# Attention with hashed buckets and two MLP blocks on one core: weight loads queued behind tile transposes, hash products in four column strips

## The chip, the cores and the metric

The kernel runs on one core of one Trainium2 chip. The time is device microseconds of one execution, the lower the better.

## The reference

Attention over 2 batches, 8 heads, 768 tokens, 64 numbers a head; a query sees the keys whose hash bucket is its own. Then a Fourier mixing with an MLP (weights w_ch1, w_ch2), then a gated MLP. The inputs are float32. The part around the change:

```python
q_bits = (np.einsum('bhsd,dk->bhsk', q, proj) > 0).astype(np.int64)
k_bits = (np.einsum('bhsd,dk->bhsk', k, proj) > 0).astype(np.int64)
mask = np.sum(q_bits * powers, axis=-1)[:, :, :, None] == np.sum(k_bits * powers, axis=-1)[:, :, None, :]
scores = np.where(mask, scale * np.matmul(q, k.transpose(0, 1, 3, 2)), -1000000000.0)
attn = np.exp(scores - np.max(scores, axis=-1, keepdims=True))
attn = attn / (np.sum(attn, axis=-1, keepdims=True) + 1e-09)
return np.matmul(attn, v)
...
un = (u - mu) / np.sqrt(var + 1e-06)
return u + np.maximum(un @ w_ch1, 0.0) @ w_ch2
```

## The kernel before

The 96 attention tiles (2 batches x 8 heads x 6 tiles of 128 queries) are worked one after the other by `attention`. For a tile, TensorE forms the scores (L387) into a tile s, VectorE takes their maximum (L397), ScalarE the exponential e (L399). Then e is split into an fp16 pair: a cast (L246, in batch 0 on GpSimd) and a subtract (L251, GpSimd); SyncE issues a transpose of the pair by DMA (L438), and three tiles later TensorE multiplies the result with V (L455 to L457). In batch 0, tiles 1 and 4 of each head go another way (`flip`): TensorE transposes e (L423).

Before a head, `prep_head` and `stacks` make its operands: q1 is a copy of x (queries above keys) scaled by qsc (L248 on VectorE, or L246 on GpSimd, as ENG says), k2 the remainder x qsc - q1 on VectorE (L258); three moves by DMA (L266) and one on GpSimd (L246) put the halves where TensorE wants them. Every two heads, `prep_group` loads x and v and forms the hash products z = zp x (L304, float32, each product in two passes), of which ScalarE takes the sign (L273); a product with the code table gives ct (L353), and ScalarE writes two blocks of rows from it (L280, L282) by which wrong buckets drop out of the scores.

`weight` prepares an MLP matrix. The matrices w1 and w2 hold 64-bit floats: a piece of them is loaded as pairs of 32-bit words into a buffer `wide` (L215, on SyncE's queue, 1 MB for w1, 512 KB for w2), VectorE turns it into float32 in three steps (L219, L220, L221), ScalarE sums the squares (L223), and at the end ScalarE and VectorE write the fp16 pair (L232, L234). There are three buffers `wide` for w1 and two for w2. w1 runs beside batch 0, w2 beside batch 1, w_in and w_out beside the second MLP product of batch 1.

`build` interleaves these streams by weights (`_merge`), and the framework's scheduler orders each engine's instructions from that; an engine runs its own in that order, and SyncE's queue carries every load, move and transpose. s, ct, z and the tile tp of `flip` share one ring of two-bank PSUM buffers (three in batch 0, two later); `pp` is a pool of one-bank tiles.

Of the kernel before, what the change touches and what calls it, by code (L numbers as in the profile page):

```python
# [9 lines left out]
F32 = mybir.dt.float32  # L10
FR = mybir.dt.float32r
F16 = mybir.dt.float16
I32 = mybir.dt.int32
AF = mybir.ActivationFunctionType
ALU = mybir.AluOpType
# [3 lines left out]
B, H, S, D = 2, 8, 768, 64  # L19
DM, DF, DG = 512, 2048, 1024  # L20
P = 128
NT = S // P
HT = NT // 2
HS = S // 2
NB = 6
GH = 2
# [22 lines left out]
NX = 4  # L49
W3 = 0.4  # L50
PEND = 5
BITS = 'A'
WB = (3, 2)
ENG = ({'oh': 'A', 'hi': 'D', 'mv': 'SSPS', 'cast': 'P', 'sub': 'P'}, {'oh': 'A', 'hi': 'P', 'mv': 'SSPS', 'cast': 'AAP', 'sub': 'P'})
GP = ''
FULL = (3, 11)
ZP = (False, False)
CP = (False, False)
ENG0 = {'hi': 'D', 'mv': 'AASA', 'oh': 'A'}
W_ATT0 = 1.5  # L60
# [41 lines left out]
class Kern:  # L102
    def __init__(self, tc, I, out):
        self.tc, self.nc, self.I, self.out = tc, tc.nc, I, out
        self.W = {}


    def rsqrt(self, pool, x, n):
# [42 lines left out]
    def setup(self, ctx):  # L151
        tc, nc, I = self.tc, self.nc, self.I
        self.cp = cp = ctx.enter_context(tc.tile_pool(name="const", bufs=1))
        self.ident = cp.tile([P, P], F32, tag="ident", name="ident")
        self.ones = cp.tile([P, P], F32, tag="ones", name="ones")
        self.codes = cp.tile([P, GH, P], F16, tag="codes", name="codes")
        self.pops = cp.tile([P, 2], F32, tag="pops", name="pops")
        pr = cp.tile([P, NB], F32, tag="pr", name="pr")
        nc.scalar.dma_start(out=pr, in_=I["proj"])
        nc.scalar.dma_start(out=self.codes, in_=I["codes"])  # L160
        nc.scalar.dma_start(out=self.pops, in_=I["pops"])
        nc.scalar.dma_start(out=self.ident, in_=I["ident"])
        self.zp = cp.tile([P, GH, 2 * GH * NB], F32, tag="zp", name="zp")
        nc.vector.memset(self.zp, 0.0)
        for hl in range(GH):
            for n in range(2):
                r = slice(64 * n, 64 * n + 64)
                o = NB * (2 * hl + n)
                nc.vector.tensor_copy(self.zp[r, hl, o:o + NB], pr[r])
        self.bits = []  # L170
        for i in range(2):
            t = cp.tile([P, S], F16, tag=f"bits{i}", name=f"bits{i}")
            nc.gpsimd.memset(t, 0.0)
            self.bits.append(t)
        nc.vector.memset(self.ones, 1.0)
        self.qsc = cp.tile([P, 1], F32, tag="qsc", name="qsc")
        nc.vector.memset(self.qsc[0:64], SCALE)
        nc.vector.memset(self.qsc[64:128], 1.0)
        self.XU = [cp.tile([P, NT, DM], F32, tag=f"xu{b}", name=f"xu{b}") for b in range(B)]

        def col(n):
            return cp.tile([P, 1], F32, tag=n, name=n)

        self.sc = {nm: (col(f"s_{nm}"), col(f"i_{nm}")) for nm in ("w1", "w2", "in", "sg", "out")}
        self.sg_ = [[(col(f"sv{b}{g}"), col(f"iv{b}{g}")) for g in range(NG)] for b in range(B)]
        self.iv1 = [[col(f"iw{b}{g}") for g in range(NG)] for b in range(B)]
        for t in sum(self.iv1, []):
            nc.gpsimd.memset(t[64:65], 1.0)
        self.sx = [(col(f"sx{b}"), col(f"ix{b}")) for b in range(B)]
        self.vq = [cp.tile([P, NG], F32, tag=f"vq{b}", name=f"vq{b}") for b in range(B)]  # L190
        self.prod = col("prod")
        self.tok = [cp.tile([P, NT], F32, tag=f"tok{b}", name=f"tok{b}") for b in range(B)]
        self.tiny = col("tiny")
        nc.gpsimd.memset(self.tiny, -1e-37)


    def weight(self, pool, nm, src, regions, spare, c, q):

        nc = self.nc
        wide = src.dtype == mybir.dt.int64  # L200
        src = src.bitcast(I32) if wide else src
        sub = WSUB.get(nm, 4)
        m = c // sub
        n = len(regions)
        s, i = self.sc[nm]
        acc = pool.tile([P, 8], F32, tag="wacc", name="wacc", bufs=1)
        tot = pool.tile([P, 1], F32, tag="wm", name="wm", bufs=1)
        for j in range(n):
            if not wide:
                q.dma_start(out=regions[j], in_=src[:, j * c:(j + 1) * c])  # L210
                yield 0.3
            for hf in range(sub if wide else 0):
                o = j * c + hf * m
                x = self.stp.tile([P, 2 * m], I32, tag="wide", name="wide", bufs=self.wb)
                q.dma_start(out=x, in_=src[:, 2 * o:2 * (o + m)])  # L215
                xv = x.rearrange("p (n w) -> p n w", w=2)
                lo, hi = xv[:, :, 0], xv[:, :, 1]
                t = regions[j][:, hf * m:(hf + 1) * m].bitcast(I32)
                nc.vector.tensor_scalar(out=t, in0=hi, scalar1=3, scalar2=0x3FFFFFFF, op0=ALU.logical_shift_left, op1=ALU.bitwise_and)  # L219
                nc.vector.scalar_tensor_tensor(out=t, in0=hi, scalar=-0x40000000, in1=t, op0=ALU.bitwise_and, op1=ALU.bitwise_or)  # L220
                nc.vector.scalar_tensor_tensor(out=t, in0=lo, scalar=29, in1=t, op0=ALU.logical_shift_right, op1=ALU.bitwise_or)  # L221
                yield 0.0029 * m
            nc.scalar.activation(spare[:, 0:c], regions[j], AF.Square, accum_out=acc[:, j:j + 1])  # L223
            yield 0.0005 * c
        nc.vector.tensor_reduce(tot, acc[:, 0:n], axis=AX.X, op=ALU.add)
        self.norm_pow2(tot, 2.0 ** 54, s, i, self.pc if nm == "w2" else None)
        yield 1.0
        views = []
        dst = spare
        for j in range(n):  # L230
            d = dst[:, 0:c].bitcast(F16).rearrange("p (t c) -> p t c", t=2)
            nc.scalar.activation(d[:, 0, :], regions[j], AF.Copy, scale=i)  # L232
            yield 0.0005 * c
            nc.vector.scalar_tensor_tensor(out=d[:, 1, :], in0=regions[j], scalar=i, in1=d[:, 0, :], op0=ALU.mult, op1=ALU.subtract)  # L234
            views.append(d)
            dst = regions[j]
            yield 0.0005 * c
        self.W[nm] = views
        self.spare = dst
# [28 lines left out]
                self.copy(e, to.bitcast(FR), fr)  # L268
        return (q1, k1), (q2, k2)

    def to_bits(self, out, z):
        if BITS == "A":
            self.nc.scalar.activation(out, z, AF.Sign, bias=self.tiny[0:24])  # L273
        else:
            self.nc.vector.tensor_scalar(out=out, in0=z, scalar1=0.0, scalar2=None, op0=ALU.is_gt)

    def one_hot(self, eng, qo, ko, c):

        nc = self.nc
# [6 lines left out]
    def prep_group(self, ap, vp, n, G):  # L286

        nc, I = self.nc, self.I
        b, g = divmod(n, NG)
# [6 lines left out]
        nc.sync.dma_start(out=v, in_=I["v"][b, g])  # L296
        yield
        bits = self.bits[n % 2]
        to = bits[0:24].rearrange("p (a c) -> p a c", a=2)
        z = None if ZP[b] else self.ps.tile([P, 2, 512], F32, tag="s", name="z")  # L300
        for hf in range(2):
            zh = self.pp.tile([P, 512], F32, tag="p", name="z")[:, 0:HS] if ZP[b] else z[:, hf, 0:HS]
            for hl in range(GH):
                nc.tensor.matmul(zh[0:24], self.zp[:, hl, :], xs[hl][:, hf * HS:(hf + 1) * HS], start=hl == 0, stop=hl == GH - 1)  # L304
            if ZP[b]:
                self.to_bits(to[:, hf], zh[0:24])
        if not ZP[b]:
            self.to_bits(to, z[0:24, :, 0:HS])
        yield
        vf = v.rearrange("p a b c -> p (a b) c")[:, :, 0:64]  # L310
        V = ap.tile([P, GH, NT, 130], F16, tag="V", name="V", bufs=2)
# [48 lines left out]
    def attention(self, ap, eps):  # L360

        nc = self.nc
# [66 lines left out]
        def rest(i):  # L429
            if flips(i):  # L430
                flip(i)
                return
            x = st[i]
            ep, EB = pick(i)
            c = ENG[i // (H * NT)]["sub"]
            self.sub(c[i % len(c)], x["eh"][:, 1, :], x["e"], x["eh"][:, 0, :])
            x["et"] = et = ep.tile([P, 2 * NT, P], F16, tag="et", name="et", bufs=EB[2])
            nc.sync.dma_start_transpose(out=et, in_=x["eh"].rearrange("p a c -> p (a c)"))  # L438

        def av(i):  # L440
            g, hl, qt = where(i)
# [373 lines left out]
    def build(self):  # L815
# [3 lines left out]
        with ExitStack() as ctx:  # L819
# [48 lines left out]
            def second():  # L868
                yield from att
                c_att.close()  # L870
                c_s2.close()
                pp3 = c_ps.enter_context(tc.tile_pool(name="pp3", bufs=4, space=PSUM))
                self.pp = Alt(pp, pp3, pp3, pp2, pp3, pp3)
                up = ctx.enter_context(tc.tile_pool(name="up", bufs=1))
# [31 lines left out]
def _tables():  # L906
# [22 lines left out]
    codes = np.zeros((P, GH, P), np.float16)  # L929
    sign = np.where((np.arange(64)[None, :] >> np.arange(NB)[:, None]) & 1, 1.0, -1.0)  # L930
    for hl in range(GH):
        codes[12 * hl:12 * hl + 6, hl, 0:64] = sign
        codes[12 * hl + 6:12 * hl + 12, hl, 64:128] = sign
    pop = (sign > 0).sum(0).astype(np.float32)
    pops = np.zeros((P, 2), np.float32)
    if BITS == "A":
        pop = np.full_like(pop, NB)
    pops[0:64, 0] = BIG * (1.0 - pop)
    pops[64:128, 0], pops[64:128, 1] = pop, -pop
    return {  # L940
# [45 lines left out]
```

## Time and profile before

| | us |
|---|---|
| median of 3 runs | 726.32 (720.83 to 726.87) |
| profiled execution | 724.48 |
| its span | 722.7 |
| TensorE, VectorE busy | 645.0 (89%), 503.9 (70%) |
| ScalarE, GpSimd busy | 329.8 (46%), 273.7 (38%) |

The profile names engines PE (TensorE matmul), PEld (its weight loads), DVE (VectorE), ACT (ScalarE), POOL (GpSimd) and SP (SyncE). A row of a group of instructions reads: line, engine, operation, output<-inputs, shapes, count | busy us, mean ns of one | idle time of the engine before them and what ended it. A row of a timeline reads: start, length in us, then the instruction. The span ends with the last instruction; the execution's time has some 2 us around it.

### The profile page before, as it was taken

To read this page: it belongs to the slowest core of one execution; us is meant where nothing else is said; L and a number is where in the kernel's file an instruction comes from. 1 tells how busy PE (TensorE), PEld (TensorE's weight loads), DVE (VectorE), ACT (ScalarE), POOL (GpSimd) and SP (SyncE) were. 2 spreads that over 40 slices of the span, in tenths; PEclk is the share of its full clock that TensorE was granted. 3 is DMA by queue.
4 is the path that set the end of the run, shared out by engine and by line. 5 is a ranking of instruction groups with operands and counts; after the bars stand their busy time and mean duration, and the time that the engine had idled before them with its cause. 6 is when DMAs were issued, how large, how long until landed. Compare 5 with 4: busy or idle time off the path is not lost.

```text
span 722.7 us, 12521 instructions
## 1 busy us (share of the span) xinstructions
PE 645.0 (89%) x4828; PEld 421.8 (58%) x4828; DVE 503.9 (70%) x1095; ACT 329.8 (46%) x517; POOL 273.7 (38%) x232
## 2 busy tenths in 40 slices
PE   3788987976876578999999999979999999999997
PEld 0666677764563357658865766736668444444443
DVE  6999598658999997745435694867562266777663
ACT  5766687764664556745632421423642044222110
POOL 2568588879486465536455041000000012111000
PEclk8899999996886879999999999989999999999999
DMA  8969787999798989737563036552000012011334
GB/s 310 312 182 213 140 175 143 204 202 259 158 235 169 212 193 211 140 67 152 101 128 108 2 60 221 125 148 91 1 1 1 1 35 53 15 29 18 86 88 117
DMA packets 182428, 92.24 MB, mean 128 GB/s; under 512 B 166240, under 2 KB 167008, under 8 KB 181344
## 3 DMA queue, kind: packets, MB, share of 16 engines
q1 hardware_dynamic: 181792, 91.30, 55.0%
q8 instruction: 38, 0.62, 0.4%
q10 hardware_dynamic: 576, 0.14, 0.1%
q14 instruction: 22, 0.18, 0.1%
HBM read 39.50 MB, written 3.15 MB: 59 GB/s over the span
## 4 chain that ended last, share of the span: by engine, by line
PE 56%; DVE 21%; DMA 12%; POOL 4%; issue 3%; ACT 2%; SPq 0%; DVEq 0%; POOLq 0%; ACTq 0%
PE c L674 13%; PE c L657 12%; PE gi L739 9%; PE sg L762 6%; PE s L387 4%; PE go L779 4%; DMA wide<-w_in 3%; DMA et<-eh 3%; DMA wide<-w 3%; DVE nm L397 2%; DVE w L221 2%; DVE w L220 2%; POOL eh L251 2%; DVE k L258 1%; PE y L542 1%
## 5 line engine op out<-in xcount | busy, mean ns | idle before, releaser
L251 POOL TENSOR_TENSOR eh<-e,eh 128x768 f16<-128x768 f32 x80 | 143.4, 1796 | 53.7 <-ACT eh L244 51.0
L657 PE MATMUL c<-unT,w 128*128 128x256 f16 x1152 | 136.8, 277 | 4.2 <-DVE h L664 4.2
L674 PE MATMUL c<-w,h 128*128 128x512 f16 x576 | 131.8, 384 | 5.3 <-DVE xu L678 5.3
L657 PEld LDWEIGHTS <-w 128*128 128x128 f16 x1152 | 113.0, 99 | 22.6 <-issue 5.3
L387 PE MATMUL s<-k,q 128*128 128x384 f32 x384 | 108.1, 413 | 17.8 <-ACT k L282 7.4
L399 ACT ACTIVATE e<-s,nm 128x768 f32<-128x768 f32 x96 | 85.3, 896 | 55.3 <-DVE nm L397 44.7
L397 DVE TENSOR_REDUCE nm<-s 128x1 f32<-128x768 f32 x96 | 90.3, 948 | 22.6 <-PE s L387 21.5
L674 PEld LDWEIGHTS <-h 128*128 128x128 f16 x576 | 56.2, 99 | 69.6 <-issue 9.2
L755 POOL TENSOR_TENSOR vh<-gv,vh 128x512 f16<-128x512 f32 x12 | 13.9, 1156 | 214.0 <-ACT vh L754 214.0
L387 PEld LDWEIGHTS s<-k,q 128*128 128x128 f32 x384 | 72.0, 211 | 30.1 <-ACT k L282 8.3
L455 PE MATMUL pav<-V,et 128*128 128x65 f16 x480 | 56.4, 199 | 19.2 <-DMA et<-eh 13.8
L664 DVE SCALAR_TENSOR_TENSOR h<-c,h 128x256 f16<-128x256 f32 x96 | 39.8, 419 | 36.3 <-ACT h L663 35.8
L246 POOL TENSOR_SCALAR eh<-e 128x768 f16<-128x768 f32 x48 | 47.9, 999 | 36.8 <-ACT e L399 30.7
L455 PEld LDWEIGHTS <-et 128*128 128x128 f16 x480 | 46.0, 102 | 26.1 <-DMA et<-eh 17.7
L456 PE MATMUL pav<-V,et 128*128 128x64 f16 x480 | 56.2, 197 | 0.0
L457 PE MATMUL pav<-V,et 128*128 128x65 f16 x480 | 56.2, 199 | 0.0
L456 PEld LDWEIGHTS <-et 128*128 128x128 f16 x480 | 46.5, 101 | 7.7 <-issue 6.9
L739 PE MATMUL gi<-in,xT 128*128 128x512 f16 x216 | 50.5, 379 | 0.0
L663 ACT ACTIVATE h<-c 128x256 f16<-128x256 f32 x96 | 34.6, 377 | 34.6 <-PE c L657 34.2
L739 PEld LDWEIGHTS <-xT 128*128 128x128 f16 x288 | 28.2, 98 | 35.0 <-issue 1.1
L457 PEld LDWEIGHTS <-et 128*128 128x128 f16 x480 | 46.5, 101 | 1.5 <-issue 0.8
L762 PE MATMUL sg<-vh,sg 128*128 128x512 f16 x180 | 40.8, 379 | 0.0
(198 smaller groups left out, 1009.9 us busy)
## 6 DMA issues: line engine op xcount, KB each, us to landing
wide<-w SPq DMA_DIRECT2D x8, 1024.0 KB, 8.9
wide<-w SPq DMA_DIRECT2D x16, 512.0 KB, 4.3
x<-qk SPq DMA_DIRECT2D x16, 384.0 KB, 4.5
k<-q SPq DMA_DIRECT2D x26, 192.0 KB, 4.1
wide<-w_in SPq DMA_DIRECT2D x16, 256.0 KB, 3.5
vst<-v SPq DMA_DIRECT2D x8, 396.0 KB, 5.3
y<-ot SPq DMA_DIRECT2D x12, 256.0 KB, 2.3
q<-q SPq DMA_DIRECT2D x13, 192.0 KB, 3.9
```

The source lines that it names most:

```text
L246: self.nc.gpsimd.tensor_scalar(out=out, in0=src, scalar1=scale, scalar2=1.0, op0=ALU.mult, op1=ALU.mult)
L251: (self.nc.vector if eng == "D" else self.nc.gpsimd).tensor_tensor(out=out, in0=a, in1=b, op=ALU.subtract)
L387: nc.tensor.matmul(s[:, hf, 0:HS], q[:, qs], k[:, hf * HS:(hf + 1) * HS], start=n == 0, stop=n == len(pairs) - 1)
L397: nc.vector.tensor_reduce(nm, x["s"], axis=AX.XY, op=ALU.max, negate=True)
L399: nc.scalar.activation(e.rearrange("p (a c) -> p a c", a=2), x["s"], AF.Exp, bias=nm)
L455: nc.tensor.matmul(pv[:, qt, 0:65], et[:, kb, :], V[:, hl, kb, 64:129], start=kb == 0, stop=False)
L456: nc.tensor.matmul(pv[:, qt, 0:64], et[:, kb, :], V[:, hl, kb, 0:64], start=False, stop=False)
L457: nc.tensor.matmul(pv[:, qt, 0:65], et[:, NT + kb, :], V[:, hl, kb, 64:129], start=False, stop=kb == NT - 1)
L657: nc.tensor.matmul(ps[:, 0:step], w[:, a, fo], uT[:, 4 * u + kc, o * P:o * P + step], start=m == 0, stop=m == 11)
L674: nc.tensor.matmul(ps, hs[n, f][:, a, j * P:(j + 1) * P], wv[:, w, :], start=f + m == 0, stop=f == NF - 1 and m == 2)
L739: nc.tensor.matmul(ps, xT[:, 4 * a + kc, :], w_in[kc][:, w, half * DM:(half + 1) * DM], start=n == 0, stop=n == 11)
L762: nc.tensor.matmul(ps, w_sg[kt][:, w, t * P:(t + 1) * P], vh[b][:, kt, a, :], start=n == 0, stop=n == 17)
```

## The change

Loads: `weight` asks for piece k+1 before it works on piece k (for w1, w2, and also w_in and w_out, which go through the same code), and while attention runs each load is put behind the newest tile transpose in SyncE's order. Hash products: zp is now 32 columns wide, and the four products of a group write four strips of 32 partitions of one bank from `pp`; the sign is taken in two instructions of 64 partitions. The code table follows. The scaled copy q1 (and its half-height form for head 3) of batch 0 goes to GpSimd, except for head 0.

```diff
-ENG = ({'oh': 'A', 'hi': 'D', 'mv': 'SSPS', 'cast': 'P', 'sub': 'P'}, ...)
+ENG = ({'oh': 'A', 'hi': 'P', 'mv': 'SSPS', 'cast': 'P', 'sub': 'P'}, ...)
...
+        def load(k):
+            if k >= n * sub:
+                return None
+            x = self.stp.tile([P, 2 * m], I32, tag="wide", name="wide", bufs=self.wb)
+            with ExitStack() as es:
+                if self.lastT is not None:
+                    es.enter_context(self.tc.issue_after(self.lastT))
+                q.dma_start(out=x, in_=src[:, 2 * m * k:2 * m * (k + 1)])
+            return x
+
+        nxt = load(0) if wide else None
...
-                o = j * c + hf * m
-                x = self.stp.tile([P, 2 * m], I32, tag="wide", name="wide", bufs=self.wb)
-                q.dma_start(out=x, in_=src[:, 2 * o:2 * (o + m)])
+                x, nxt = nxt, load(j * sub + hf + 1)
...
-        to = bits[0:24].rearrange("p (a c) -> p a c", a=2)
-        z = None if ZP[b] else self.ps.tile([P, 2, 512], F32, tag="s", name="z")
+        z = self.pp.tile([P, 512], F32, tag="p", name="z")
         for hf in range(2):
-            zh = self.pp.tile([P, 512], F32, tag="p", name="z")[:, 0:HS] if ZP[b] else z[:, hf, 0:HS]
             for hl in range(GH):
-                nc.tensor.matmul(zh[0:24], self.zp[:, hl, :], xs[hl][:, hf * HS:(hf + 1) * HS], start=hl == 0, stop=hl == GH - 1)
-            if ZP[b]:
-                self.to_bits(to[:, hf], zh[0:24])
-        if not ZP[b]:
-            self.to_bits(to, z[0:24, :, 0:HS])
+                r = 32 * (GH * hf + hl)
+                nc.tensor.matmul(z[r:r + 32, 0:HS], self.zp, xs[hl][:, hf * HS:(hf + 1) * HS], start=True, stop=True)
+        for hf in range(2):
+            r = slice(64 * hf, 64 * hf + 64)
+            nc.scalar.activation(bits[0:64, hf * HS:(hf + 1) * HS], z[r, 0:HS], AF.Sign, bias=self.tiny[r])
...
-            nc.sync.dma_start_transpose(out=et, in_=x["eh"].rearrange("p a c -> p (a c)"))
+            self.lastT = nc.sync.dma_start_transpose(out=et, in_=x["eh"].rearrange("p a c -> p (a c)")).ins
...
                 c_s2.close()
+                self.lastT = None
```

What the change moves, by the engines' orders. First VectorE at the first tiles of batch 0, before:

```order
L221 SCALAR_TENSOR_TENSOR w_2_150<-wide,w_2_150 128x1024
L328 SCALAR_TENSOR_TENSOR V<-vst,iv_94,V 128x12x64
L219 TENSOR_SCALAR w_3_151<-wide 128x1024
L220 SCALAR_TENSOR_TENSOR w_3_151<-wide,w_3_151 128x1024
L397 TENSOR_REDUCE nm<-s 128x1
L221 SCALAR_TENSOR_TENSOR w_3_151<-wide,w_3_151 128x1024
L397 TENSOR_REDUCE nm<-s 128x1 x3
```

and in the changed kernel at the same place (line numbers are those of its own file):

```order
L229 SCALAR_TENSOR_TENSOR w_2_148<-wide,w_2_148 128x1024
L328 SCALAR_TENSOR_TENSOR V<-vst,iv_92,V 128x12x64
L397 TENSOR_REDUCE nm<-s 128x1 x6
L266 SCALAR_TENSOR_TENSOR k_508<-x,qsc,q_505 128x768
L397 TENSOR_REDUCE nm<-s 128x1
L227 TENSOR_SCALAR w_3_149<-wide 128x1024
```

The third piece of w1 (w_3) stood around the first maximum nm, and now comes after the seventh. Next SyncE's queue over the first heads, before:

```order
L215 DMA wide<-w 128x2048 x3
L438 DMA_TRANSPOSE et<-eh 128x12x128 x3
L266 DMA k_504<-q_503 64x768
L438 DMA_TRANSPOSE et<-eh 128x12x128
L266 DMA q_505<-q_503 64x768
L266 DMA k_506<-q_503 64x768
L438 DMA_TRANSPOSE et<-eh 128x12x128
L293 DMA x<-qk 128x768
L215 DMA wide<-w 128x2048 x2
```

and after:

```order
L298 DMA vst<-v 128x792 x2
L438 DMA_TRANSPOSE et<-eh 128x12x128
L214 DMA wide<-w 128x2048
L438 DMA_TRANSPOSE et<-eh 128x12x128 x2
L214 DMA wide<-w 128x2048
L274 DMA k_506<-q_505 64x768
L274 DMA q_507<-q_505 64x768
L438 DMA_TRANSPOSE et<-eh 128x12x128 x2
L274 DMA k_508<-q_505 64x768
L214 DMA wide<-w 128x2048
```

Before, six of the eight loads of w1 stand ahead of the first transpose and the other two together behind the fifth; now two stand ahead of it, and the other six singly behind the 1st, 3rd, 5th, 7th, 9th and 11th. Last GpSimd around the operands of one head, before:

```order
L246 TENSOR_SCALAR eh<-e 128x768 x2
L251 TENSOR_TENSOR eh<-e,eh 128x768 x2
L246 TENSOR_SCALAR eh<-e 128x768
L246 TENSOR_SCALAR q_505<-k_506 64x768
L251 TENSOR_TENSOR eh<-e,eh 128x768
```

and after:

```order
L254 TENSOR_SCALAR eh<-e 128x768
L254 TENSOR_SCALAR q_505<-x,qsc 128x768
L259 TENSOR_TENSOR eh<-e,eh 128x768
L254 TENSOR_SCALAR eh<-e 128x768
L254 TENSOR_SCALAR q_507<-k_508 64x768
```

The scaled copy of x, which was VectorE's L248, is now a GpSimd instruction among the casts and subtracts of the running tiles.

## Rows read from the trace of the kernel before

**Rows 1.** Stretches: from:to us, length, busy PE, PEld, DVE, ACT, POOL, PEclk, DMA, GB/s
```profile
25.00:65.00 40.00, 32.40 (x279) 25.92 (x280) 37.78 (x40) 25.60 (x38) 30.09 (x21) 0.91 0.88 213
...
85.00:125.00 40.00, 34.36 (x369) 28.99 (x367) 36.79 (x53) 32.75 (x43) 32.13 (x23) 0.96 0.78 153
165.00:280.00 115.00, 82.26 (x699) 56.45 (x699) 108.03 (x167) 60.91 (x94) 74.69 (x58) 0.80 0.92 207
280.00:722.00 442.00, 431.84 (x2964) 262.31 (x2962) 266.80 (x756) 153.69 (x267) 85.19 (x69) 0.99 0.33 77
```

**Rows 2.** Groups of VectorE's instructions, 22 to 165 us
```profile
L234 DVE SCALAR_TENSOR_TENSOR w<-w,i_w,w 128x1024 f16<-128x1024 f32 x8 | 13.7, 1718 | 0.0
L220 DVE SCALAR_TENSOR_TENSOR w<-wide,w 128x1024 int32<-128x1024 int32 x5 | 10.9, 2180 | 0.0
L221 DVE SCALAR_TENSOR_TENSOR w<-wide,w 128x1024 int32<-128x1024 int32 x6 | 9.9, 1653 | 0.0
L258 DVE SCALAR_TENSOR_TENSOR k<-x,qsc,q 128x768 fp32r<-128x768 f32 x7 | 9.6, 1365 | 0.0
L248 DVE TENSOR_SCALAR q<-x,qsc 128x768 fp32r<-128x768 f32 x5 | 7.1, 1412 | 0.1
...
L219 DVE TENSOR_SCALAR w<-wide 128x1024 int32<-128x1024 int32 x5 | 4.1, 820 | 0.5 <-DMA wide<-w 0.5
```

**Rows 3.** The tile q: count, shortest/median/longest in ns, first and last start
```profile
L258 DVE SCALAR_TENSOR_TENSOR k<-x,qsc,q x14: 1002/1018/2098, 5.4 to 333.1; 128x768 fp32r<-128x768 f32 x14
...
L246 POOL TENSOR_SCALAR q<-k x13: 823/829/1798, 8.1 to 334.7; 64x768 fp32r<-64x768 f32 x13
L248 DVE TENSOR_SCALAR q<-x,qsc x7: 612/1256/1999, 4.2 to 121.9; 128x768 fp32r<-128x768 f32 x7
L246 POOL TENSOR_SCALAR q<-x,qsc x7: 904/907/1315, 134.8 to 332.1; 128x768 fp32r<-128x768 f32 x7
```

**Rows 4.** Timeline of the first tiles, 18.5 to 24.5 us
```profile
19.04 0.69 DVE L219 TENSOR_SCALAR w<-wide 128x1024 int32<-128x1024 int32 x1 [0.84 <-DMA wide<-w]
19.77 1.23 DVE L220 SCALAR_TENSOR_TENSOR w<-wide,w 128x1024 int32<-128x1024 int32 x1
...
21.89 0.90 ACT L399 ACTIVATE e<-s,nm 128x768 f32<-128x768 f32 x1 [1.75 <-DVE nm L397]
...
24.14 0.88 ACT L399 ACTIVATE e<-s,nm 128x768 f32<-128x768 f32 x1
```

**Rows 5.** Groups of GpSimd's instructions, 22 to 165 us
```profile
L251 POOL TENSOR_TENSOR eh<-e,eh 128x768 f16<-128x768 f32 x35 | 64.9, 1860 | 1.9
L246 POOL TENSOR_SCALAR eh<-e 128x768 f16<-128x768 f32 x33 | 33.3, 1012 | 22.5 <-ACT e L399 22.4
L246 POOL TENSOR_SCALAR q<-k 64x768 fp32r<-64x768 f32 x7 | 8.0, 1145 | 9.8 <-DVE k L258 5.1 <-issue 2.4 <-PE z L304 2.4
L246 POOL TENSOR_SCALAR q<-x,qsc 128x768 fp32r<-128x768 f32 x2 | 1.8, 906 | 1.1 <-PE s L387 1.1
```

**Rows 6.** The tile eh, as rows 3
```profile
L251 POOL TENSOR_TENSOR eh<-e,eh x80: 1632/1648/2732, 23.8 to 374.9; 128x768 f16<-128x768 f32 x80
L246 POOL TENSOR_SCALAR eh<-e x48: 821/830/1808, 22.9 to 374.0; 128x768 f16<-128x768 f32 x48
```

**Rows 7.** Timeline of VectorE and GpSimd at 90 and at 103 us
```profile
90.10 1.28 DVE L234 SCALAR_TENSOR_TENSOR w<-w,i_w,w 128x1024 f16<-128x1024 f32 x1
90.34 1.72 POOL L246 TENSOR_SCALAR q<-k 64x768 fp32r<-64x768 f32 x1 [2.27 <-DVE k L258]
...
102.46 2.50 POOL L251 TENSOR_TENSOR eh<-e,eh 128x768 f16<-128x768 f32 x1
103.51 1.87 DVE L248 TENSOR_SCALAR q<-x,qsc 128x768 fp32r<-128x768 f32 x1
```

**Rows 8.** Timeline of TensorE, the second group's hash products
```profile
29.56 2.76 PE L304 MATMUL z<-x,zp 128*24 128x384 f32 x8
```

**Rows 9.** Page, DMA issues: count, KB each, median us to landing
```profile
wide<-w SPq DMA_DIRECT2D x8, 1024.0 KB, 8.9
```

More of the change, by code (lines that the diff above doesn't have):

```diff
@@ L51 @@
 PEND = 5
-BITS = 'A'
 WB = (3, 2)
-ENG = ({'oh': 'A', 'hi': 'D', 'mv': 'SSPS', 'cast': 'P', 'sub': 'P'}, {'oh': 'A', 'hi': 'P', 'mv': 'SSPS', 'cast': 'AAP', 'sub': 'P'})
+ENG = ({'oh': 'A', 'hi': 'P', 'mv': 'SSPS', 'cast': 'P', 'sub': 'P'}, {'oh': 'A', 'hi': 'P', 'mv': 'SSPS', 'cast': 'AAP', 'sub': 'P'})
 GP = ''
 FULL = (3, 11)
-ZP = (False, False)
 CP = (False, False)
@@ L162, in setup @@
         nc.scalar.dma_start(out=self.ident, in_=I["ident"])
-        self.zp = cp.tile([P, GH, 2 * GH * NB], F32, tag="zp", name="zp")
+        self.zp = cp.tile([P, 32], F32, tag="zp", name="zp")
         nc.vector.memset(self.zp, 0.0)
[L165 to L169, printed above, removed]
+        for n in range(2):
+            r = slice(64 * n, 64 * n + 64)
+            nc.vector.tensor_copy(self.zp[r, NB * n:NB * n + NB], pr[r])
         self.bits = []
@@ L269, in stacks @@
         return (q1, k1), (q2, k2)
[L271 to L275, printed above, removed]
     def one_hot(self, eng, qo, ko, c):
@@ L871, in second @@
                 c_s2.close()
+                self.lastT = None
                 pp3 = c_ps.enter_context(tc.tile_pool(name="pp3", bufs=4, space=PSUM))
@@ L931, in _tables @@
     for hl in range(GH):
-        codes[12 * hl:12 * hl + 6, hl, 0:64] = sign
-        codes[12 * hl + 6:12 * hl + 12, hl, 64:128] = sign
+        codes[32 * hl:32 * hl + 6, hl, 0:64] = sign
+        codes[32 * hl + 6:32 * hl + 12, hl, 64:128] = sign
     pop = (sign > 0).sum(0).astype(np.float32)
     pops = np.zeros((P, 2), np.float32)
-    if BITS == "A":
-        pop = np.full_like(pop, NB)
+    pop = np.full_like(pop, NB)
     pops[0:64, 0] = BIG * (1.0 - pop)
```

## The prediction

> **What bounds the kernel now.** I read the table of stretches first. In the first 165 us the attention of batch 0 runs, with w1 being unpacked beside it; up to about 280 us the attention of batch 1, the first Fourier part and the unpacking of w2; from 280 us on TensorE is busy 431.84 of 442 us [rows 1], at 0.99 of full clock. That last stretch is TensorE's own work, and the change touches little of it, so a gain must come from what ends before 280 us, and it then reaches the end whole. In 165 to 280 us VectorE is busy 108.03 of 115 us: it sets that stretch. In the batch 0 stretches no engine is full by itself: VectorE 37.78 and 36.79 of 40 us, TensorE 32.40 and 34.36, GpSimd 30.09 and 32.13 [rows 1].
>
> Next I read the groups of GpSimd and VectorE instructions between 22 us (GpSimd's first tile) and 165 us, and beside them the shortest time that each form took anywhere. The mean is far above the shortest: the scaled copy q on VectorE has a mean of 1.412 us there [rows 2] and a shortest of 0.612 [rows 3]; the second step of the unpacking has 2.180 [rows 2] against 1.23 at the start [rows 4]; GpSimd's subtract 1.860 [rows 5] against 1.632 [rows 6]. The timeline shows why. At 90.10 VectorE starts a weight remainder of 1.28 us; GpSimd's copy, started at 90.34 and of 0.82 us when alone [rows 3], ends only 1.72 us later. At 102.46 GpSimd's subtract takes 2.50, and VectorE's q copy behind it at 103.51 takes 1.87 instead of 0.61 [rows 7]. The two engines take turns: an instruction of the one stretches by the rest of the other's. VectorE's 37.78 of 40 us is therefore largely waiting for GpSimd.
>
> So I add the undisturbed times of both as one resource, for 22 to 165 us. GpSimd: 35 subtracts of 1.63, 33 casts of 0.82, 7 copies of 0.82 and 2 of 0.90 [rows 3, 5, 6], 57.1 + 27.1 + 5.7 + 1.8 = 91.7 us. VectorE, leaving out what reads scores from PSUM: 8 remainders of 1.28 [rows 2, 7], 5 and 6 unpacking steps of 1.23, 5 first steps of 0.69 [rows 2, 4], 7 remainders k2 of 1.00 and 5 copies q of 0.61 [rows 2, 3], 10.2 + 13.5 + 3.5 + 7.0 + 3.1 = 37.3 us. Together 129.0 of 143 us, 90%. I take this pair, not VectorE, as the bound of the batch 0 stage.
>
> The Trainium skill ("SBUF — State Buffer", section "Who interferes with whom") says the same and gives the reason: VectorE in its two-port modes, or with two SBUF inputs, and GpSimd share one pair of ports, and whoever starts first holds it for the whole instruction while the other fully blocks. The trace agrees (the 1.72 us copy above). By that rule the move of q to GpSimd, below, costs 1.5 us; were there no such lock, it would take 7.1 us off VectorE.
>
> **The change, part by part.** The sum is made against the profiled execution, 724.48 us with a span of 722.7; the median of the three runs shown is 726.32 (720.83 to 726.87), so this execution is 1.84 below it.
>
> *The scaled copies q of batch 0* go from VectorE to GpSimd: after the first 22 us five of them, and half a one. Each takes 0.61 from VectorE and adds 0.90 to GpSimd [rows 3], so the pair gains 5 x 0.29 = 1.5 us of work. Bounds: +1.5 where the pair is full, -7.1 where VectorE's own 5 x 1.412 [rows 2] is what ends last. I take the pair's value.
>
> *The loads of w1.* In the changed order two pieces are asked for before the first tile instead of six, and the other six one by one behind tile transposes. VectorE's third piece leaves the start: between the first scores it stood with 0.69 and 1.23 us [rows 4], and the second exponential came at 24.14, not right behind the first of 21.89 (0.90 long) [rows 4], 1.35 us of gap. With the piece and its square on ScalarE gone, and the products shorter, I take the first tiles 2.0 us earlier. Bounds: -3.5 (piece, gap and half of the products) and +1.0, since VectorE now runs the scale that hangs on the products ahead of the first piece of w1. The price: 0.69 + 1.23 = 1.9 us of unpacking that ran beside an idle GpSimd now fall into the crowded stage. With 1.5 that is +3.4 on the pair; as 10% of it is free I take half, +1.7 (bounds 0 and +3.4).
>
> *The loads of w2* are asked for one piece ahead. Both kernels have two buffers, so the third load still waits for the first piece; what changes is which transposes stand behind it in SyncE's queue. VectorE idles 115 - 108.03 = 7.0 us in that stretch [rows 1], which bounds the gain; on the other side, a load that waits holds up the transposes behind it, as now, or worse by the same 7.0. I take -2.0.
>
> *The hash products.* Four products per group, each in two passes, take 2.76 us for eight passes [rows 8], 0.345 each. They now write four different 32-column strips. The second pass of one product must follow its first, but may run beside the first pass of the next: five steps in place of eight, 1.73 us, -1.0. Bounds: two steps, -2.07 a group, and one pass more than now, +0.35. Of eight groups only the one near 297 us lies in the stretch that TensorE fills, so -1.0 counts once; the first group is in the start above, and the others fall where the pair of VectorE and GpSimd ends last. The Trainium skill ("TensorE: Matmul & The Clock Gate", section "Part 3: Packing small matmuls") gives 2.38 for three column strips: 2.76 / 2.38 = 1.16 us, an estimate from that page, 0.6 less than mine; no row here shows two strips at once. ScalarE's sign becomes two instructions of half the length: ScalarE waits in the stage, and the second one's fixed part is hidden there; it would cost some 0.1 us a group without that cover. That the products leave the ring of score buffers for the single-bank one I cost at nothing: the ring then serves scores alone, and the other bank is used only by the few tiles transposed on TensorE.
>
> The rest is unchanged work; the stretch from 280 us moves as a whole. Sum: -2.0 + 1.7 - 2.0 - 1.0 = -3.3, so 724.5 - 3.3 = **721 us**.
>
> **Rivals.**
>
> *VectorE itself is the bound.* Its 92 to 94% in two stretches of batch 0 [rows 1] speak for it; against it speak the stretched times [rows 3, 7]. Then the five copies take 5 x 1.412 = 7.1 us with them and nothing is added: -2.0 - 7.1 - 2.0 - 1.0, 712 us.
>
> *The loads get between the transposes (slower).* Six pieces of 1 MB now travel among the transposes of batch 0, against two now. Such a load took 8.9 us to land [rows 9], a subtract, and so a transpose, comes every 143 / 35 = 4.1 us [rows 5], and all share one queue. A transpose behind a load then lands up to 8.9 - 4.1 = 4.8 us later; TensorE takes a tile three tiles on, which hides perhaps half. Four loads more x 2.4 = 9.6 us: 721 + 9.6, 731 us. It decides from the point where a transpose lands more than two spacings, 8.2 us, after it is issued. Against it: each load stands right behind a transpose, so it has a whole spacing before the next.
>
> *The products do not run side by side.* Then the strips bring nothing, and the start is lost too, because the scale ahead of the first unpacking waits for them: -2.0 and -1.0 fall away, +1.7 and -2.0 stay, 724 us, no change. The passes of one product bind each other, which speaks for it.
>
> **How the numbers follow.** Forecast 0.45, VectorE alone 0.22, loads between transposes 0.18, no strips side by side 0.15. About 1% (7.2 us) is what a measurement of this kernel can tell from no change. Of the forecast's own spread, 716 to 726 us, I give a quarter of its chance to over 1% faster and a twentieth to over 1% slower; nine tenths of the second case are faster; seven tenths of the third are slower; of the last nearly all lies within. Faster: 0.11 + 0.20 = 0.31; slower: 0.02 + 0.13 + 0.02 = 0.17; the same 0.52. For eight in ten the range goes from 709, a little below the second case, to 733, a little above the third; it holds the bounds of the single terms too.
>
> **What would show it.** Right: the second exponential directly behind the first; the q copies on GpSimd near 0.90 us, VectorE's k2 behind them stretched; batch 0 ending within 3 us of 165; eight passes of the products in under 2 us; the last stretch as long as now. Wrong: batch 0 ending before 158 us (VectorE was the bound), TensorE's wait for transposed tiles grown by several us (the loads), or the eight passes still 2.7 us. A change of more than 3 us in the stretch behind 280 us would be something that I have not seen.

## The result and the profile after

The changed kernel takes 728.71 us (median of 11 runs, 727.05 to 732.16), the kernel before 722.22 on the same chip (11 runs, 719.61 to 729.18). The ratio is 1.0082, 95% interval 1.0057 to 1.0106: some 6 us slower, where 721 us had been forecast. The profiled execution of the changed kernel took 728.53 us with a span of 726.7, so the two profiles differ by 4.05 us, some six tenths of what the medians differ by. What follows compares one execution of each, and executions of one kernel lie some us apart, so it places those 4.05 us and not the whole loss. The mean granted clock of TensorE is 0.943 in the profiled execution before and 0.948 in the changed one: a lower clock does not explain the loss.

The stretches of the changed kernel that answer to [rows 1], and below them TensorE's waits behind 285 us (us, times, longest):

```profile
25.00:65.00 40.00, 29.30 (x296) 26.55 (x295) 37.62 (x38) 25.00 (x37) 27.30 (x23) 0.87 1.07 238
85.00:125.00 40.00, 31.40 (x343) 27.74 (x343) 33.48 (x51) 33.91 (x45) 31.07 (x25) 0.91 0.79 159
165.00:280.00 115.00, 79.14 (x698) 55.09 (x695) 110.60 (x166) 65.93 (x99) 78.55 (x59) 0.78 0.97 211
280.00:722.00 442.00, 431.60 (x2956) 262.09 (x2954) 266.81 (x755) 153.02 (x267) 82.48 (x68) 0.99 0.35 76
```

```profile
PE c L674 <- DVE xu L678: 5.5, 2, 4.7
PE pav L455 <- DMA et<-eh: 3.1, 2, 2.6
PE y L542 <- DMA cs<-cos_s: 0.9, 1, 0.9
PE gi L739 <- DVE xu L678: 0.8, 1, 0.8
```

The same waits of the kernel before:

```profile
PE c L674 <- DVE xu L678: 5.3, 2, 4.4
PE gi L739 <- DVE xu L678: 0.8, 1, 0.8
```

Marks read from the starts of the tiles say where the time came in. The first score maximum starts at 19.46 us instead of 20.91; the first Fourier sum `fe`, taken here as the end of batch 0, starts at 164.4 instead of 164.9; the last piece of w2 starts at 278.9 instead of 278.5; the first product of the second MLP layer at 289.3 instead of 288.9. From there to the end it is 437.4 us instead of 433.8. So of 1.45 us won at the start 0.95 were lost again before 165 us, another 0.9 in the next stage, and 3.6 in the stretch that TensorE fills, where its waits behind 285 us grew from 6.1 to 10.3 us.

The pieces of the change themselves, in the order of [rows 4], [rows 8], [rows 2] and [rows 5]. First the two exponentials at the start, then the hash products of the second group:

```profile
20.46 0.90 ACT L399 ACTIVATE e<-s,nm 128x768 f32<-128x768 f32 x1 [0.50 <-DVE nm L397]
21.73 0.90 ACT L399 ACTIVATE e<-s,nm 128x768 f32<-128x768 f32 x1 [0.38 <-DVE nm L397]
...
29.99 0.85 PE L305 MATMUL z<-x,zp 128*32 128x384 f32 x8
```

VectorE's and GpSimd's groups between 22 and 165 us:

```profile
L242 DVE SCALAR_TENSOR_TENSOR w<-w,i_w,w 128x1024 f16<-128x1024 f32 x8 | 13.5, 1682 | 1.2 <-ACT w L240 1.1
L266 DVE SCALAR_TENSOR_TENSOR k<-x,qsc,q 128x768 fp32r<-128x768 f32 x7 | 11.3, 1619 | 1.2 <-POOL q L254 1.2
L228 DVE SCALAR_TENSOR_TENSOR w<-wide,w 128x1024 int32<-128x1024 int32 x6 | 10.7, 1777 | 0.1
L229 DVE SCALAR_TENSOR_TENSOR w<-wide,w 128x1024 int32<-128x1024 int32 x6 | 10.1, 1690 | 0.0
L227 DVE TENSOR_SCALAR w<-wide 128x1024 int32<-128x1024 int32 x6 | 9.8, 1640 | 2.5 <-DMA wide<-w 2.5
```

```profile
L259 POOL TENSOR_TENSOR eh<-e,eh 128x768 f16<-128x768 f32 x35 | 60.9, 1741 | 1.9
L254 POOL TENSOR_SCALAR eh<-e 128x768 f16<-128x768 f32 x33 | 32.7, 994 | 23.7 <-ACT e L399 23.7
L254 POOL TENSOR_SCALAR q<-x,qsc 128x768 fp32r<-128x768 f32 x7 | 8.9, 1265 | 0.8 <-issue 0.8
L254 POOL TENSOR_SCALAR q<-k 64x768 fp32r<-64x768 f32 x7 | 6.7, 957 | 8.0 <-DVE k L266 4.0 <-DVE wm L136 2.8 <-PE pav L457 1.2
```

The copies q have left VectorE, but the first unpacking step now takes 9.8 us for six pieces (4.1 for five in [rows 2]), and VectorE waits 2.5 us for their landing (0.5 there). The products take 0.85 us instead of 2.76 and free 7.6 us of TensorE in the four groups of this stretch; none of it shows in the time.

### The profile page after: what moved, and what is told of

Same layout as the page of the kernel before. It is cut to its first block, busy times and chain, and to the rows that moved or that the text cites. A ratio compares the mean times of both kernels' runs of the same rounds, so it can differ in the third digit from the quotient of the medians.

```text
span 726.7 us, 12549 instructions
## 1 busy us (share of the span) xinstructions
PE 631.0 (87%) x4828; PEld 416.2 (57%) x4828; DVE 508.4 (70%) x1086; ACT 334.4 (46%) x525; POOL 279.4 (38%) x239
## 4 chain that ended last, share of the span: by engine, by line
PE 50%; DVE 24%; DMA 12%; POOL 6%; issue 4%; ACT 3%; SPq 0%; POOLq 0%; DVEq 0%; ACTq 0%
PE c L657 11%; PE c L674 11%; PE gi L739 9%; PE sg L762 6%; DMA et<-eh 5%; PE go L779 4%; DVE nm L397 3%; PE s L387 3%; DMA wide<-w 3%; DMA wide<-w_in 3%; POOL eh L259 3%; DVE w L228 2%; DVE w L229 2%; DVE w L227 2%; DVE un L631 2%
## 5 line engine op out<-in xcount | busy, mean ns | idle before, releaser
L259 POOL TENSOR_TENSOR eh<-e,eh 128x768 f16<-128x768 f32 x80 | 139.7, 1748 | 52.0 <-ACT eh L252 49.3
L657 PE MATMUL c<-unT,w 128*128 128x256 f16 x1152 | 138.4, 279 | 7.6 <-DVE h L664 7.6
L455 PE MATMUL pav<-V,et 128*128 128x65 f16 x480 | 55.7, 198 | 26.1 <-DMA et<-eh 16.5
L455 PEld LDWEIGHTS <-et 128*128 128x128 f16 x480 | 45.5, 101 | 42.2 <-DMA et<-eh 23.8
L457 PE MATMUL pav<-V,et 128*128 128x65 f16 x480 | 55.0, 198 | 0.0
L456 PEld LDWEIGHTS <-et 128*128 128x128 f16 x480 | 46.0, 100 | 1.4 <-issue 0.5
L457 PEld LDWEIGHTS <-et 128*128 128x128 f16 x480 | 46.0, 100 | 0.4
```

The costliest lines, as they stand in the source:

```text
L259: (self.nc.vector if eng == "D" else self.nc.gpsimd).tensor_tensor(out=out, in0=a, in1=b, op=ALU.subtract)
L455: nc.tensor.matmul(pv[:, qt, 0:65], et[:, kb, :], V[:, hl, kb, 64:129], start=kb == 0, stop=False)
L456: nc.tensor.matmul(pv[:, qt, 0:64], et[:, kb, :], V[:, hl, kb, 0:64], start=False, stop=False)
L457: nc.tensor.matmul(pv[:, qt, 0:65], et[:, NT + kb, :], V[:, hl, kb, 64:129], start=False, stop=kb == NT - 1)
L657: nc.tensor.matmul(ps[:, 0:step], w[:, a, fo], uT[:, 4 * u + kc, o * P:o * P + step], start=m == 0, stop=m == 11)
```

## The experiments

The theories. **A**: the loads make the loss. **B**: the copies on GpSimd do. **C**: the hash products do, with their strips or their other pool of PSUM buffers. Three parts are alone or left out in eight kernels; the kernel before and the changed one are two of them.

**Each part alone, and two together.** The edits are the diff's own pieces on the kernel before; the fourth is the changed kernel with one letter back:

```diff
-ENG = ({'oh': 'A', 'hi': 'P', ...
+ENG = ({'oh': 'A', 'hi': 'D', ...
```

> The kernel before with the new loads of the weights alone (asked for one piece ahead, queued behind the newest tile transpose); hash products and scaled copies as before. Theory A (the loads make the loss): 726 to 728 us against 722.2 of the kernel before, with TensorE waiting 2 to 4 us behind 285 us for transposed tiles, as it does not in the kernel before. Theory B (the scaled copies on GpSimd make it): 720 to 722. Theory C (the hash products' new bank and strips make it): 720 to 722.

> The kernel before with the new hash products alone (four column strips, one bank of the other pool, the sign in two instructions). Each group of eight passes should take 0.85 us, as it does in the changed kernel. Theory A (loads): 720 to 721, since the group near 297 us saves 1.9 us of TensorE and the start some 1 us. Theory B (copies): the same 720 to 721. Theory C (the strips make the loss): 726 to 728.

> The kernel before with the scaled copies of batch 0 on GpSimd alone. Theory A (loads) and theory C (strips): 722 to 724, the pair of VectorE and GpSimd gaining 1.5 us of work in batch 0. Theory B (the copies make the loss): 726 to 728, with batch 0 ending 4 us later than 164.9.

> The changed kernel with the scaled copies of batch 0 back on VectorE. Theory A (loads): 726 to 728, as the changed kernel. Theory B (copies): 719 to 721. Theory C (strips): 726 to 728, and then the run with the strips alone is as slow.

Measured: loads 738.39 us, strips 734.25, copies 726.20, loads and strips 735.90, against 724.43 of the kernel before. None of A, B and C is borne out. Loads and strips are each slower alone than the whole change is. With the loads alone TensorE has none of the waits for transposed tiles behind 285 us that A asked for. The copies alone have B's time (726 to 728), but batch 0 ends earlier in them (162.7 us), not 4 us later. And the copies, put on top of loads and strips, take time away (1.0156 to 1.0082). They do it in a stage they don't touch: batch 0, where the copies stand, takes (from the first maximum) 145.5 us with loads and strips and 145.0 in the changed kernel, but the next stage, to the last piece of w2, takes 120.7 and 114.4.

That pointed to the order. The framework's scheduler orders each engine's instructions anew for every program. By the traces, one part alone puts 8 to 19% of an engine's instructions out of the order of the kernel before (what lies outside the longest common sequence). Hence theory **D**: each edit mainly draws a new order, and that of the kernel before is a good one; against it **E**: the parts cost what they add, and the order is worth little.

**The same instructions in another order.** Four edits each change one weight of the interleaving and nothing else, on the kernel before (where they move 1 to 12% of an engine's instructions) and on the changed one:

```diff
-W_ATT0 = 1.5
+W_ATT0 = 1.55
...
-W2 = 0.6
+W2 = 0.58
...
-W2 = 0.6
+W2 = 0.62
...
-W1 = (0.8, 0.3, 1.0)
+W1 = (0.82, 0.3, 1.0)
```

> The kernel before with nothing changed but one weight of the interleaving (attention of batch 0 against w1: 1.5 to 1.55): the same instructions in another order. Theory D (the orders decide: each part of the change mainly draws a new order, and that of the kernel before is a good one): 727 to 738 us against 724.4. Theory E (the parts cost what they add in work and waits, and the order is worth little): 722 to 726.

> The kernel before with one weight of the interleaving changed (w2 against the rest: 0.6 to 0.58). Theory D: 727 to 738 us. Theory E: 722 to 726.

> The kernel before with one weight of the interleaving changed (w2 against the rest: 0.6 to 0.62). Theory D: 727 to 738 us. Theory E: 722 to 726.

> The kernel before with one weight of the interleaving changed (attention of batch 1 against the Fourier part: 0.8 to 0.82). Theory D: 727 to 738 us. Theory E: 722 to 726.

> The changed kernel with one weight of the interleaving changed (attention of batch 0 against w1: 1.5 to 1.55). Theory D (orders decide): anywhere from 718 to 738 us, on either side of the changed kernel's 728.7. Theory E (the parts cost what they add): 727 to 731.

> The changed kernel with one weight of the interleaving changed (w2 against the rest: 0.6 to 0.58). Theory D: 718 to 738 us. Theory E: 727 to 731.

> The changed kernel with one weight of the interleaving changed (w2 against the rest: 0.6 to 0.62). Theory D: 718 to 738 us. Theory E: 727 to 731.

> The changed kernel with one weight of the interleaving changed (attention of batch 1 against the Fourier part: 0.8 to 0.82). Theory D: 718 to 738 us. Theory E: 727 to 731.

| run | us, median | ratio to before | 95% interval |
|---|---|---|---|
| before, attention of batch 0 at 1.55 | 728.12 | 1.0068 | 1.0039 to 1.0098 |
| before, w2 at 0.58 | 729.19 | 1.0081 | 1.0054 to 1.0108 |
| before, w2 at 0.62 | 727.88 | 1.0071 | 1.0036 to 1.0106 |
| before, attention of batch 1 at 0.82 | 728.86 | 1.0065 | 1.0035 to 1.0094 |
| after, attention of batch 0 at 1.55 | 734.74 | 1.0119 | 1.0038 to 1.0199 |
| after, w2 at 0.58 | 731.72 | 1.0112 | 1.0078 to 1.0146 |
| after, w2 at 0.62 | 731.07 | 1.0101 | 1.0072 to 1.0129 |
| after, attention of batch 1 at 0.82 | 730.16 | 1.0083 | 1.0046 to 1.0120 |

For the kernel before D is borne out: E had 722 to 726 us, and four orders without any edit to the work cost 0.65 to 0.81%, about what the change cost. For the changed kernel the two theories are not parted as clearly: one order (730.16) lies in E's 727 to 731, two lie within 0.8 us above it, one, of three runs, 3.7 above, and none came below the changed kernel. Over five orders of either kernel (its own and the four) the mean ratio is 1.0057 for before and 1.0099 for after, 1.0071 and 1.0104 over the four alone. By this reckoning the change costs 0.3 to 0.4%, 2 to 3 us, and about half of the measured 0.82% is the order of the kernel before, which the change gave up. The granted clock is no rival here: its mean over the runs is 0.950 in the kernel before and 0.947 to 0.949 in its four orders.

TensorE's waits behind 285 us point the same way. This is the kernel before with w2 at 0.58:

```profile
PE pb L136 <- issue: 4.7, 1, 4.7
PE c L657 <- DVE h L664: 1.7, 2, 1.5
PE c L674 <- DVE xu L678: 0.8, 1, 0.8
PE gi L739 <- DVE xu L678: 0.8, 1, 0.8
PE c L674 <- DVE w L234: 0.6, 1, 0.6
PE c L674 <- ACT w L232: 0.3, 1, 0.3
```

That is 8.9 us of waits, against 6.1 with its own order; the three others have 8.3 to 10.0. But these waits alone do not make the loss: two kernels below that are level with the kernel before (the strips in the ring with a free order, the copies in the old order) have 8.1.

**Parts in the order of the kernel before.** Here each engine's order is written out as the scheduler gave it for the kernel before. A list of places per engine is kept in the kernel, and after the last instruction each one is tied behind its predecessor, in issue order alone; what a part adds is left free:

```diff
+def pin(tc, nc, free):
+    for e, order in ORDER.items():
...
+        mine = [mine[n + d] for n, d in enumerate(order)]
+        for a, b in zip(mine, mine[1:]):
+            tc.add_manual_dep(b, a.name, mybir.DependencyInfo(mybir.DependencyClass.NoSync, ...
```

For the strips z stays in the ring of score buffers (in the other pool, as I read the old order, z and other tiles would wait for each other's bank for ever; no run shows it); a run with that edit and a free order stands beside it. The loads can't be put into the old order either: VectorE would unpack pieces ahead of tiles behind whose transposes their loads have to stand. So strips in the other pool, and loads, were not tried in that order.

```diff
-        z = self.pp.tile([P, 512], F32, tag="p", name="z")
+        z = self.ps.tile([P, 2, 512], F32, tag="s", name="z")
...
-                nc.tensor.matmul(z[r:r + 32, 0:HS], ...
+                nc.tensor.matmul(z[r:r + 32, 0, 0:HS], ...
```

> The kernel before with the hash products in four column strips, sign in two, but kept in the ring of score buffers; the scheduler orders freely. Theory D (orders decide): somewhere from 724 to 738 us, not below the kernel before. Theory C (it was the move into the other pool that made the run with the strips alone slow): 720 to 722.

> The same instructions as in the run before this one, but every engine's order is written out as the scheduler gave it for the kernel before (the second half of the sign stands right behind the first). Theory D: 719 to 722 us, the strips' own gain of 1 to 4 us (1.9 us of TensorE near 297 us, up to 1.5 at the start) and nothing lost. Theory C (strips or two signs cost in themselves): as slow as without the order, 728 or more.

> The kernel before with the scaled copies of batch 0 on GpSimd, all other instructions in the order of the kernel before, the copies placed by the scheduler. The prediction's term (VectorE and GpSimd share one pair of ports, the pair is full): 723 to 725 us, 0 to 1.5 above the kernel before. VectorE alone as the bound: 716 to 719.

> Strips and copies together in the order of the kernel before. Theory D with the prediction's terms: 720 to 724 us, the sum of the two runs before it; at or below the kernel before, and below the changed kernel by 5 us or more. If the parts themselves cost: 728 or more.

| run | us, median | ratio to before | 95% interval |
|---|---|---|---|
| strips in the ring, free order | 724.40 | 0.9999 | 0.9976 to 1.0022 |
| strips in the ring, old order | 727.37 | 1.0048 | 1.0019 to 1.0077 |
| copies, old order | 723.89 | 1.0010 | 0.9993 to 1.0027 |
| strips and copies, old order | 727.22 | 1.0043 | 1.0021 to 1.0066 |

The copies came out as expected in time, at +0.7 us. The strips did not, alone or with the copies: D expected 719 to 722 and 720 to 724 us, the old order should have kept their gain, and they lost 0.5% in it. So keeping the order does not keep the time. The same strips are level with the kernel before in the ring with a free order (D had it above, C below) and at 1.0128 in the other pool; that the pool itself costs this is not shown, as strips and copies in that pool, below, are at 1.0026. What happens to the freed time is seen from 22 to 165 us. First the stretch in the kernel before and with the strips in its order, columns as [rows 1]:

```profile
22.00:165.00 143.00, 121.80 (x1148) 98.55 (x1147) 114.61 (x148) 103.62 (x141) 109.69 (x87) 0.93 0.90 192
```

```profile
22.00:165.00 143.00, 113.92 (x1140) 94.21 (x1139) 110.93 (x145) 103.14 (x142) 107.36 (x85) 0.93 0.90 190
```

Then TensorE's two largest waits there, in the same two kernels (us, times, longest):

```profile
PE pav L455 <- DMA et<-eh: 10.7, 9, 2.7
PE tp L423 <- ACT e L399: 2.7, 3, 1.8
```

```profile
PE pav L463 <- DMA et<-eh: 14.3, 10, 3.1
PE tp L431 <- ACT e L407: 7.8, 5, 3.7
```

TensorE's work falls by 7.9 us and these waits, for tiles and for exponentials, rise by 8.7. In a stretch of fixed length idle time must rise as work falls; that the saving is waited out and more is seen at its end: the first `fe` starts at 167.2 us instead of 164.9, the first product of the second MLP layer at 291.3 instead of 288.9, and the span is 725.2 instead of 722.7. So nearly all of this profile's loss lies before 165 us, at the same granted clock (0.93 in both rows). The sign, in two instructions, takes 2 x 0.575 instead of 0.875 us:

```profile
L273 ACT ACTIVATE bits<-z,tiny x8: 875/876/892, 10.5 to 300.0; 24x768 f16<-24x768 f32 x8
```

```profile
L314 ACT ACTIVATE bits<-z,tiny x16: 558/575/579, 7.8 to 303.0; 64x384 f16<-64x384 f32 x16
```

Over its nine runs this kernel also shows a lower mean clock than the kernel before beside it, 0.942 against 0.950, and its longest run (733.84 us) the lowest, 0.932; how much of the 0.48% that makes in the runs without a trace, and whether it is a cause or follows from the waits, is open.

How a small shift grows is seen at 53 us. VectorE and GpSimd in the kernel before, and then in the same order with the strips, where VectorE waits for a piece of w1 and starts on it 0.4 us later:

```profile
53.95 0.69 DVE L219 TENSOR_SCALAR w<-wide 128x1024 int32<-128x1024 int32 x1
54.56 1.01 DVE L328 SCALAR_TENSOR_TENSOR V<-vst,iv,V 128x768 f16<-128x768 f32 x1
55.49 1.84 DVE L220 SCALAR_TENSOR_TENSOR w<-wide,w 128x1024 int32<-128x1024 int32 x1
...
54.66 1.61 POOL L246 TENSOR_SCALAR eh<-e 128x768 f16<-128x768 f32 x1 [1.87 <-ACT e L399]
56.35 2.50 POOL L251 TENSOR_TENSOR eh<-e,eh 128x768 f16<-128x768 f32 x1
```

```profile
54.33 0.69 DVE L233 TENSOR_SCALAR w<-wide 128x1024 int32<-128x1024 int32 x1 [0.47 <-DMA wide<-w]
54.94 1.58 DVE L336 SCALAR_TENSOR_TENSOR V<-vst,iv,V 128x768 f16<-128x768 f32 x1
56.44 2.66 DVE L234 SCALAR_TENSOR_TENSOR w<-wide,w 128x1024 int32<-128x1024 int32 x1
...
54.66 1.05 POOL L260 TENSOR_SCALAR eh<-e 128x768 f16<-128x768 f32 x1 [1.87 <-ACT e L407]
55.80 2.22 POOL L265 TENSOR_TENSOR eh<-e,eh 128x768 f16<-128x768 f32 x1
```

GpSimd's cast starts at 54.66 in both. In the first VectorE's remainder is ahead of it by 0.10 us and runs in 1.01, and the cast stretches to 1.61; in the second the cast is ahead, is done in 1.05, and VectorE pays: 1.58, then 2.66. The next maximum on VectorE comes 1.76 us later (59.02 against 57.26), out of a shift of 0.4. This is the lock of the Trainium skill ("SBUF — State Buffer", section "Who interferes with whom"), by which the one that starts first holds the shared ports, and the trace agrees: which engine pays turns on a tenth of a microsecond.

This shift is not yet the loss. Five tiles on it is gone (the 19th maximum comes 0.2 us earlier than in the kernel before), and it comes and goes until 131 us. The lag that stays, 2.9 us at the 42nd maximum and 2.5 at the last, comes with one wait for a transposed tile, in the kernel before and then with the strips:

```profile
133.54 0.20 PE L455 MATMUL pav<-V,et 128*128 128x65 f16 x1 [0.79 <-DMA et<-eh]
```

```profile
135.52 0.20 PE L463 MATMUL pav<-V,et 128*128 128x65 f16 x1 [2.38 <-DMA et<-eh]
```

GpSimd was 0.35 us behind with the pair just before; why the transposes then landed that much later is open.

The copies in the old order show the other half. Batch 0 ends 3.0 us earlier in them (161.9), and the last maximum still starts 2.6 us earlier (369.4 against 372.0), but the span is only 0.8 us shorter (721.9). The rest went in the stretch that TensorE fills, in the same order, where one of its waits is new:

```profile
PE c L677 <- DVE h L684: 2.6, 1, 2.6
```

**The last two combinations.** Theory **F**: the loads have a cost of their own that outlasts the orders. The edits are again whole pieces of the diff, taken out of the changed kernel.

> The changed kernel with the loads as before (neither asked for ahead nor queued behind the transposes). Theory F (the loads cost some 6 to 8 us of their own, whatever the order): 720 to 724 us, that is at least 5 below the changed kernel. Theory D (each combination is a draw): 724 to 738, with no need to be below the changed kernel.

> The changed kernel with the hash products as before. Theory F: 730 to 736 us, at least 5 above the run with the copies alone (726.2). Theory D: 724 to 738, with no need to be above it.

Strips and copies took 725.80 us, ratio 1.0026 (0.9998 to 1.0055); loads and copies 732.43, ratio 1.0132 (1.0100 to 1.0163). The first lies in D's range (724 to 738 us), not in F's (720 to 724), though 0.56% below the changed kernel; the second lies where F had it (730 to 736), which is in D's range too, 1.04% above the copies alone. All eight, with marks of the profiled executions (us; "wait" is VectorE's idle time ahead of w1's first steps from 22 to 165 us, put down to the landing):

| loads, strips, copies | ratio | batch 0 ends | wait | w2's first step | w2's last piece |
|---|---|---|---|---|---|
| none (before) | 1 | 164.9 | 0.5 | 182.6 | 278.5 |
| strips | 1.0128 | 167.6 | 0.7 | 185.9 | 288.7 |
| copies | 1.0028 | 162.7 | 0.0 | 175.4 | 275.4 |
| strips, copies | 1.0026 | 169.7 | 0.0 | 187.2 | 280.0 |
| loads | 1.0180 | 169.1 | 2.9 | 193.9 | 292.2 |
| loads, strips | 1.0156 | 165.5 | 3.3 | 187.7 | 286.2 |
| loads, copies | 1.0132 | 170.3 | 3.7 | 196.7 | 284.2 |
| all (after) | 1.0082 | 164.4 | 2.5 | 189.4 | 278.9 |

Each part is seen in four pairs. Loads: +1.80, +0.28, +1.04, +0.56%, mean +0.92%. Strips: +1.28, -0.02, -0.24, -0.50, mean +0.13%. Copies: +0.28, -1.02, -0.48, -0.74, mean -0.49%. The spread of each set of four, 1.3 to 1.8 points, is wider than what a weight alone moved (0.81 points in the kernel before, 0.37 in the changed one), so orders of that size, or parts that act on each other, stand behind it; no run parts the two. Only the loads are on one side four times, once (+0.28%) within the noise of the two runs: F's sign is likely, not shown; its size, 7 us on the mean with 2 to 13 in the single pairs, is not steady as F had it. In all four kernels with the new loads VectorE waits some 3 us for w1's pieces, as the third piece is asked for at 25.6 us in the changed kernel (at 8.4 in the kernel before), and w2's first step comes 9.1 us later on the mean of four (191.9 against 182.8). First VectorE's first step on the pieces of w1 with the loads alone, the kernel before standing in [rows 2]; then the first step on w2, before and with the loads alone:

```profile
L230 DVE TENSOR_SCALAR w<-wide 128x1024 int32<-128x1024 int32 x6 | 5.5, 920 | 2.9 <-DMA wide<-w 2.9
```

```profile
182.62 0.41 DVE L219 TENSOR_SCALAR w<-wide 128x512 int32<-128x512 int32 x1
```

```profile
193.90 0.40 DVE L230 TENSOR_SCALAR w<-wide 128x512 int32<-128x512 int32 x1
```

That last row shows no wait for the landing, so its delay need not be the load's; it can be the order's. The sum of w1's squares, too, comes at 86 to 90 us with the new loads and at 68 to 82 without them, and TensorE waits for what follows it in those four kernels alone (1.2 to 5.2 us). That all this makes the 7 us is argued from the marks, not shown: no run gave the early loads back while all else stood still. No version beat the kernel before; the strips in the ring with a free order and the copies in the old order are level with it.

## Why the prediction was wrong, point by point

**The step that failed** is the path: "so a gain must come from what ends before 280 us, and it then reaches the end whole", and with it "The rest is unchanged work; the stretch from 280 us moves as a whole". It does not move as a whole. In the changed kernel the work there is the same, but TensorE's waits behind 285 us grew from 6.1 to 10.3 us (3.1 for transposed tiles, 0.9 for a table of the Fourier part), which no part of the sum had, and the stretch from 289 us took 3.6 us longer. Even in the old order the 2.6 us that the copies had won at the last maximum were 0.8 at the end (one execution of each). Nor had the sum a term for the order: with no edit to the work the kernel before loses 0.65 to 0.81% (4.7 to 5.9 us) in four other orders, more than the whole forecast sum of 3.3 us. The sign "A change of more than 3 us in the stretch behind 280 us would be something that I have not seen" is what came. How much of the loss is order and how much the parts' own cost stays open: the averages over orders leave 2 to 3 us to the parts.

**The start, -2.0.** The mechanism was right, with -1.45 for the first maximum and two exponentials 1.27 us apart instead of 2.25. But by the 13th tile the changed kernel stood 0.9 us behind (53.87 against 52.93), and no more than 0.5 us of it reached the end of batch 0.

**The scaled copies, 1.5 of the 3.4 of which half, +1.7, was taken.** In the old order the copies cost 0.10% (0.7 us; -0.07 to +0.27%), which is their half of 1.5. That is luck: the pair was to become slower in batch 0, and batch 0 ended 3.0 us earlier; the time went later. The sign "q copies near 0.90 us on GpSimd, k2 stretched" came half: k2 went from 1.365 [rows 2] to 1.619, but the copies too were stretched, to 1.265. Over four pairs the part gained 0.49% on the mean, one pair of the four losing. The forecast of VectorE alone (712 us) did not come either. The sum of undisturbed times had also left out the four remainders V (4.7 us busy in that stretch, 1.0 each alone), which take turns with GpSimd at 54 us, so the pair was booked for 133 of 143 us. That batch 0 would end within 3 us of 165 held (164.4).

**The w2 loads, -2.0.** The term had the wrong sign. Asked for one piece ahead but tied behind a transpose, the loads came later, not earlier: the first of w2 is issued at 180.7 us instead of 170.1. The loads as a whole, those of w1 with them, cost 0.92% on the mean, 6.7 us; no run has those of w2 alone.

**The hash products, -1.0.** I took the second pass of one product to run beside the first of the next. All four strips run side by side: eight passes in 0.85 us, two steps, the lower bound (-1.91 of -2.07). No gain is seen in the time, even in the old order: what TensorE saved in batch 0 ahead of tiles and exponentials it waited out, and what became of the group near 297 us was not followed. That "-1.0 counts once" was too much. The sign in two instructions costs 2 x 0.575 - 0.875 = 0.28 us a group, not some 0.1.

**The rivals.** "The loads get between the transposes" came nearest in time (731) but not by its mechanism: TensorE's waits for transposed tiles from 22 to 165 us fell, from 10.7 to 8.9 us:

```profile
PE pav L455 <- DMA et<-eh: 8.9, 8, 2.4
PE pav L455 <- DVE xu L464: 6.2, 3, 5.5
PE pb L135 <- DVE wm L233: 5.2, 1, 5.2
```

The second and third rows are what grew instead: waits for VectorE, the second of them for what follows the sum of w1's squares, which comes at 88.1 us instead of 71.5 with the later loads. "No strips side by side" fell; "VectorE alone" fell by its time, though the copies in the old order did shorten batch 0, as it and not the forecast had it. That VectorE and GpSimd take turns stands (the rows at 54 us); that the sum of their undisturbed times bounds batch 0 does not fit the 3.0 us: in the rows at 54 us what counts is who starts first.

## What to carry to other kernels

Where a scheduler orders the program, change one weight that adds no work and measure that before believing a few microseconds of an edit; here such a change cost 0.65 to 0.81% in the kernel before and up to 0.4% in the changed one, and an edit can lose a tuned order. Compare means over several orders of both kernels. Writing the old order out for the new instructions is a second check, not a proof: the strips lost 0.5% in the old order and nothing in a free one. Saved time on an engine counts only where nothing else is late behind it: in the old order the strips took 7.9 us of work off TensorE in batch 0, and batch 0 ended 2.3 us later.

## What the runs showed that I had not expected

Four column strips of float32 products, two passes each, run in 0.85 us instead of 2.76, that is 3.2 times as fast; the Trainium skill ("TensorE: Matmul & The Clock Gate", section "Part 3: Packing small matmuls") gives 2.38 for three strips, and no run here had three. Executions of one kernel lie further apart than I had taken: 725.39 to 733.73 us for one of the reordered kernels, so a single pair of profiles can't tell 4 us. Two traces of other orders are of runs at the ends of their nine, w2 at 0.62 of the longest (733.73) and attention of batch 1 at 0.82 of the shortest (723.91), and both show more waits behind 285 us than the kernel before.
